# Moving the bounds' matmuls, one evacuation and the norms of a fused attention and feed-forward kernel

## The chip, the cores and the metric

One core of one Trainium2 chip runs the kernel. The metric is the time on the device of one execution in microseconds; lower is better. The engines are TensorE (PE, its weight loads PEld), VectorE (DVE), ScalarE (ACT), GpSimd (POOL) and SyncE (SP), which here issues DMAs.

## The reference

Attention over 4 batches and 8 heads with pooled queries, then a normalised feed-forward with a residual:

```python
# q, k, v: (4, 8, 1152, 64) f32;  w_ch1: (512, 2048);  w_ch2: (2048, 512)
q_pool = q.reshape(B, H, S // 2, 2, D).mean(axis=3)
scores = scale * np.matmul(q_pool, k.transpose(0, 1, 3, 2))
attn = np.exp(scores - np.max(scores, axis=-1, keepdims=True))
attn = attn / (np.sum(attn, axis=-1, keepdims=True) + 1e-09)
x = np.matmul(attn, v)            # then (B, 576, 512)
xn = (x - mu) / np.sqrt(var + 1e-06) * g_ln
out = x + np.maximum(xn @ w_ch1, 0.0) @ w_ch2
```

## The kernel before, in words

**Steps.** Two heads of one batch are a pair `p` (16 pairs, 4 to a batch, `HP` = 4), and a pair has 9 steps of 128 query rows against 1152 keys (`C` = 9), so 144 steps `i`, followed by some 20 that only finish. The order in which each engine gets its instructions is written out by hand in `step(i)`: what it calls first stands first in an engine's queue. `early` and `todo` hold what is to be done at the start or at the end of a given step (`pre`, `at`).

**Attention in a step.** `emit_s(i + 1)` computes the next step's scores into a slot of three PSUM banks (line 380 for 1024 keys, 388 for the last 128; the slots of even and odd steps are banks 0 to 2 and 3 to 5). Keys and queries are split into a high and a low fp16 part, so three products are summed. `emit_max` reduces the row maximum (399), `emit_exp` exponentiates (413). In the first batch (`on_pe`, steps 0 to 35) the probabilities stay fp32: TensorE transposes them (446), ScalarE copies them out (452), TensorE multiplies with the values (470), and the 65-row result is turned back (498, `emit_turn`). From step 36 on the probabilities are split into two fp16 parts: `emit_hi` on ScalarE (427), `emit_lo` on VectorE (436) or, in every third step, on GpSimd (254, 434); one transposing DMA on SP (439) turns them, and four steps later TensorE multiplies them with the split values (482). Such a result lies in the third bank of the next step's slot.

**Evacuation.** `evac_pv` gives two closures: `one` takes the reciprocal of the row sums on VectorE (530, or 532 and 533), `two` scales the 64 columns out of PSUM into the row buffer on ScalarE (537). In the first batch `one` goes to `found`, which is run at the start of the next step right after the maximum, and `two` to `scaled_out`, which is run after that step's exponential. Later both go to `evacs`, which `flush` runs after the scores of the step.

**Banks and evacuations.** Two banks (6 and 7) serve everything else: pieces of keys and queries (`prep_k`, `prep_q`), units of the feed-forward and the norms' transposes. `bank()` takes a free one; if there is none it runs `flush()`, which issues all evacuations that wait.

**Bounds and scales.** Each pair needs a power of two for keys, queries and values. `bound` sums absolute values per partition on ScalarE (190). `scales_reduce` puts two closures into `reds`, one to a step: `one` transposes the accumulators (206), and in the next step's flush VectorE takes the maximum (209) and multiplies it with the identity (210); `two` spreads it over the partitions by a small matmul (215), and in the flush after that `scales` makes the factors (235 to 250). Both matmuls write the third bank of the next step's slot, other columns. From step 36 on `step` issues them right after the next scores and the split, ahead of the product with the values, the pieces and the unit.

**Preparations.** While pair `p - 1` runs, pair `p` is prepared; with `i0` the first step of pair `p - 1`, the loads go out near `i0`, the bounds at `i0` to `i0 + 2`, the reduction at `i0 + 2` or `i0 + 3`, and the pieces from `i0 + 4` on, one a step, in the order of `PREPS` (each is transposed on TensorE, lines 294, 298, 323, 333; then high part on ScalarE, 283 or 308, low part on VectorE, 280 or 303). From pair 6 on the queries of two pairs are prepared together with the even pair, which then has two more pieces. Raw keys and raw values have one buffer each. All loads go through SP's queue, in order.

**Feed-forward.** When a batch's 128-row tile is complete, `evacuated` appends it to `norms`; `norm(i)` takes one a step: mean and variance on VectorE (563, 564), the scaling on GpSimd (569 to 575), and two steps later four transposes on TensorE (581) with evacuations on ScalarE and VectorE (587, 588). Two normalised tiles give `units`, one of which TensorE does in each step (`some_units`): first layer 24 matmuls (618, evacuated at 631 and 632), second layer 8 to 12 matmuls (650, evacuated at 663). What is left when step 143 is done makes the tail.

**Order in a step from 36 on:** maximum, `found`, scores of the next step, `flush`, exponential, high part, low part of the step before, `norm`, one of `reds`, product with the values, piece, unit, `todo`.

## Time and profile before

| | us |
|---|---|
| median of 3 runs (lowest, highest) | 913.89 (908.51, 914.88) |
| the profiled execution | 909.41 |
| its span, first to last instruction | 907.4 |
| mean granted TensorE clock | 0.983 |
| TensorE busy | 826.9 (91%) |
| VectorE busy | 624.7 (69%) |
| ScalarE busy | 569.6 (63%) |
| GpSimd busy | 361.6 (40%) |

The profile is of one execution. Busy time is the share of the span in which the engine ran an instruction; a wait is idle time ahead of an instruction, put down to the semaphore that came last. Steps 0 to 35 run from 16.0 to 203.7 us, 36 to 53 to 303.9, 54 to 142 to 778.2, counted from one maximum to the next; the rest is the last step and the tail.

### The profile page before, as it was taken

The page shows a single profiled execution, that of the slowest core. Times are in us where ns is not written, and L with a number is a line of the kernel's source. Part 1 is how long each engine was busy: PE and PEld are TensorE (multiplying, and loading weights), DVE is VectorE, ACT ScalarE, POOL GpSimd, SP SyncE. Part 2 cuts the span into 40 slices and gives each one's busy share as a digit, 9 for nine tenths or more (in the row PEclk, how much of TensorE's full clock was granted, in tenths as well). Part 3 has the DMA queues.
Part 4 walks back from the last instruction along what each step waited for, and adds up shares of the span by engine and source line. Part 5 has one row for each costly group of instructions (what it writes and reads, how often), then busy time and mean ns, then how long its engine had stood idle before and what let it go on. Part 6 is the DMA issues. An engine that isn't in the chain of part 4 may idle for free.

```text
span 907.4 us, 21663 instructions
## 1 busy us (share of the span) xinstructions
PE 826.9 (91%) x9180; PEld 584.8 (64%) x9180; DVE 624.7 (69%) x1087; ACT 569.6 (63%) x850; POOL 361.6 (40%) x324
## 2 busy tenths in 40 slices
PE   8998897998789988797999999898989999999997
PEld 6787776776546564654666666466657576766764
DVE  3688989797877786576777777877777777641211
ACT  4998696887657756566766667576767766511110
POOL 3020927257859726262633334444624342400000
PEclk9999899899999999898999999999999999999999
DMA  7374425304676877776796969587888876600001
GB/s 191 136 213 127 148 84 163 119 26 94 121 163 129 185 140 143 164 155 136 147 176 114 194 134 186 111 179 132 162 157 147 162 129 131 131 20 12 13 12 24
DMA packets 276017, 115.97 MB, mean 128 GB/s; under 512 B 259280, under 2 KB 259280, under 8 KB 275920
## 3 DMA queue, kind: packets, MB, share of 16 engines
q1 hardware_dynamic: 275568, 113.70, 59.2%
q8 instruction: 72, 1.18, 0.6%
q10 hardware_dynamic: 352, 0.88, 0.4%
q14 instruction: 25, 0.20, 0.1%
HBM read 46.14 MB, written 4.72 MB: 56 GB/s over the span
## 4 chain that ended last, share of the span: by engine, by line
PE 40%; DVE 31%; ACT 16%; DMA 5%; issue 5%; POOL 2%; SPq 0%; ACTq 0%; POOLq 0%; DVEq 0%
PE psum L650 12%; PE psum L618 10%; DVE mx L399 9%; DVE hl L436 6%; ACT pe L413 4%; PE psum L470 4%; PE psum L482 4%; DMA pt<-hl 3%; PE psum L380 3%; DVE ht L632 3%; PE psum L446 2%; DVE stage L111 2%; ACT ht L631 2%; ACT qt L283 2%; DVE dg L210 1%
## 5 line engine op out<-in xcount | busy, mean ns | idle before, releaser
L413 ACT ACTIVATE pe<-psum,nb,sc 128x1152 f32<-128x1152 f32 x144 | 188.9, 1312 | 36.8 <-DVE nb L404 26.1
L399 DVE TENSOR_REDUCE mx<-psum 128x1 f32<-128x1152 f32 x144 | 194.3, 1349 | 25.3 <-PE psum L482 12.9
L650 PE MATMUL psum<-wsl,ht 128*128 128x512 f16 x864 | 197.8, 381 | 1.9 <-DVE xb L663 0.8
L618 PEld LDWEIGHTS <-wsl 128*128 128x128 f16 x1920 | 172.6, 99 | 24.1 <-issue 4.4
L618 PE MATMUL psum<-xn,wsl 128*128 128x256 f16 x1536 | 180.3, 276 | 1.5 <-DVE ht L632 0.8
L650 PEld LDWEIGHTS <-ht 128*128 128x128 f16 x864 | 83.0, 98 | 92.3 <-issue 4.7
L427 ACT ACTIVATE hl<-pe 128x1152 f16<-128x1152 f32 x108 | 125.7, 1163 | 9.8 <-DMA pt<-hl 6.5
L380 PE MATMUL psum<-kt,qt 64*128 64x512 f16 (+1 forms) x960 | 121.8, 380 | 3.2 <-ACT pe L413 2.3
L482 PE MATMUL psum<-vt,pt 128*128 128x65 f16 (+1 forms) x3240 | 118.4, 194 | 0.0
L482 PEld LDWEIGHTS <-pt 128*128 128x128 f16 (+1 forms) x3240 | 110.3, 101 | 2.3 <-issue 0.2
L436 DVE SCALAR_TENSOR_TENSOR hl<-pe,hl 128x1152 f16<-128x1152 f32 x72 | 108.8, 1512 | 3.5 <-ACT hl L427 3.5
L537 ACT ACTIVATE xb<-psum,r 128x64 f32<-128x64 f32 x128 | 39.4, 308 | 113.7 <-DVE r L533 110.3
L254 POOL TENSOR_SCALAR pe<-pe 128x1152 f32<-128x1152 f32 x36 | 42.1, 1169 | 163.0 <-ACT hl L427 151.0
L632 DVE SCALAR_TENSOR_TENSOR ht<-psum,ht 128x512 f16<-128x512 f32 x72 | 49.7, 690 | 75.1 <-ACT ht L631 74.7
L631 ACT ACTIVATE ht<-psum 128x512 f16<-128x512 f32 x72 | 42.8, 594 | 88.9 <-PE psum L618 88.7
L434 POOL TENSOR_TENSOR hl<-pe,hl 128x1152 f16<-128x1152 f32 x36 | 86.4, 2399 | 3.0
L470 PE MATMUL psum<-pt,vt 128*65 128x128 f32 (+1 forms) x720 | 80.5, 269 | 1.4 <-DVE qt L280 1.4
L470 PEld LDWEIGHTS psum<-pt,vt 128*65 128x65 f32 x720 | 74.6, 142 | 1.8 <-DVE qt L280 1.8
L380 PEld LDWEIGHTS <-qt 64*128 64x128 f16 (+1 forms) x960 | 34.3, 96 | 55.7 <-issue 36.2
L388 PEld LDWEIGHTS <-qt 128*128 128x128 f16 (+1 forms) x320 | 17.9, 99 | 72.5 <-issue 72.0
L280 DVE SCALAR_TENSOR_TENSOR qt<-psum,s,qt 128x512 f16<-128x512 f32 (+2 forms) x43 | 28.5, 663 | 42.7 <-ACT qt L283 42.7
L388 PE MATMUL psum<-kt,qt 128*128 128x128 f16 (+1 forms) x320 | 41.4, 226 | 12.1 <-ACT xb L537 10.5
(119 smaller groups left out, 1021.9 us busy)
## 6 DMA issues: line engine op xcount, KB each, us to landing
stage<-in_moe_w_ch_dram SPq DMA_DIRECT2D x32, 512.0 KB, 5.1
kr<-in_k_dram SPq DMA_DIRECT2D x16, 576.0 KB, 4.7
qraw<-in_q_dram SPq DMA_DIRECT2D x31, 288.0 KB, 5.0
vr<-in_v_dram SPq DMA_DIRECT2D x15, 576.0 KB, 4.9
out_dram<-xb SPq DMA_DIRECT2D x32, 128.0 KB, 2.4
pt<-hl SPq DMA_TRANSPOSE x108, 4.6
kr<-in_k_dram SPq DMA_DIRECT2D x16, 64.0 KB, 4.3
vr<-in_v_dram ACTq DMA_DIRECT2D x1, 576.0 KB, 6.8
```

What stands on the lines that cost most here:

```text
L380: nc.tensor.matmul(out=sp[o:o + w, c0:c0 + 512], lhsT=qt[r:r + 64, qa, c:c + w], rhs=kt[r:r + 64, ka, h], start=(a == 0), stop=(a == 2),)
L399: nc.vector.tensor_reduce(mx, st["s"], axis=AX.X, op=ALU.max)
L413: nc.scalar.activation(out=st["pe"], in_=st["s"], func=ACTF.Exp, scale=pair[i // C]["sc"][:, 0:1], bias=st["nb"],)
L427: nc.scalar.activation(out=hl[:, 0], in_=st["pe"], func=ACTF.Copy, scale=2.0 ** 15)
L434: nc.gpsimd.tensor_tensor(hl[:, 1], st["pe"], hl[:, 0], op=ALU.subtract)
L436: nc.vector.scalar_tensor_tensor(hl[:, 1], st["pe"], 2.0 ** 15, hl[:, 0], op0=ALU.mult, op1=ALU.subtract)
L470: nc.tensor.matmul(out=ps[0:65, q0:q0 + w], lhsT=vt[:, h, c], rhs=pt[:, 128 * u + q0:128 * u + q0 + w], start=(u == 0), stop=(u == C - 1),)
L482: nc.tensor.matmul(out=dst[:, 0:n], lhsT=lhsT, rhs=rhs, start=(u == 0 and lhsT is hi and n == 65), stop=(u == C - 1 and lhsT is lo), skip_ ...
L618: nc.tensor.matmul(out=ps[:, o:o + n], lhsT=wsl[:, 8 * w + cc, wa, f * 128:f * 128 + 128], rhs=xn[:, xa * KD + cc, 0:n], start=(m == 0), s ...
L631: lambda: nc.scalar.activation(out=hi, in_=pv, func=ACTF.Relu),
L632: lambda: nc.vector.scalar_tensor_tensor(lo, pv, 0.0, hi, op0=ALU.max, op1=ALU.subtract),
L650: nc.tensor.matmul(out=ps, lhsT=hv[0][:, ha, f, t * 128:t * 128 + 128], rhs=wsl[:, 8 * w + 4 + f // 2, wa, (f % 2) * DM:(f % 2) * DM + DM] ...
```

## The change

- In `all_max`, the product of line 210 is one operation on the PSUM block: maximum of the block's n columns and `mx`, times the identity. As `mx` is the row's maximum the value is the same.
- In the first batch `two` runs on VectorE, and directly behind `one`; `scaled_out` is gone.
- From step 54 on (`JOINT * C`), a bound's matmul is issued behind the feed-forward's unit of its step instead of ahead of the product with the values.
- `norm` leaves a batch's third and fourth tile, and the half tiles, until the sixth step of a pair or later.
- Pair 5 prepares its second key piece last, two steps later than before, and its last two query pieces stay where they were. From pair 6 on, an even pair's last two query pieces come one step later.
- Pair 6's keys are loaded two steps later, its values one, and its key bound is one step later. The other pairs' times stay.

```diff
--- before.py
+++ after.py
@@ -207,7 +207,9 @@
 
             def evac():
                 nc.vector.tensor_reduce(mx[0:n], ps[0:n], axis=AX.X, op=ALU.max)
-                nc.vector.tensor_scalar(dg[0:n, 0:n], ident[0:n, 0:n], mx[0:n], None, op0=ALU.mult)
+                nc.vector.scalar_tensor_tensor(
+                    dg[0:n, 0:n], ps[0:n, 0:n], mx[0:n], ident[0:n, 0:n], op0=ALU.max, op1=ALU.mult
+                )
             return evac
 
         def two():
@@ -339,6 +341,8 @@
     PREPS = ((prep_k, 0), (prep_k, 2), (prep_q, 0), (prep_k, 1), (prep_q, 1), (prep_q, 2))
 
     def preps_of(p):
+        if p == JOINT - 1:
+            return PREPS[:3] + PREPS[4:] + PREPS[3:4]
         if p < JOINT:
             return PREPS
         if p % 2:
@@ -487,7 +491,7 @@
                     )
         return ps
 
-    turned, scaled_out = deque(), deque()
+    turned = deque()
 
     def emit_turn(n, ot, i):
 
@@ -497,8 +501,7 @@
         for h, q0, w in parts:
             nc.tensor.transpose(ps[0:w, 65 * h:65 * h + 65], ot[:, q0:q0 + w], ident[0:65, 0:65])
         one, two = evac_pv(n, ps)
-        found.append(one)
-        scaled_out.extend((two, lambda: evacuated(n)))
+        found.extend((one, two, lambda: evacuated(n)))
 
     pv_slot = [0]
     xb, xh = {}, {}
@@ -534,10 +537,11 @@
 
         def two():
             for u in range(m):
-                nc.scalar.activation(
-                    out=x[:, 64 * u:64 * u + 64], in_=ps[o:o + n, 65 * u:65 * u + 64],
-                    func=ACTF.Copy, scale=r[:, u:u + 1],
-                )
+                src, dst = ps[o:o + n, 65 * u:65 * u + 64], x[:, 64 * u:64 * u + 64]
+                if on_pe(i):
+                    nc.vector.tensor_scalar(dst, src, r[:, u:u + 1], None, op0=ALU.mult)
+                else:
+                    nc.scalar.activation(out=dst, in_=src, func=ACTF.Copy, scale=r[:, u:u + 1])
 
         return one, two
 
@@ -832,10 +836,10 @@
         if old:
             lk = max(i0 - 1, 0)
         else:
-            lk = i0 - 2 if p % 2 or not ahead else i0 - 3
+            lk = i0 - 3 * ahead + p % 2
         at(lk, load, p, "k", nc.sync)
-        at(i0 - ahead, load, p, "v", nc.sync)
-        at(i0 + 1 if old else i0, bound, p, "k")
+        at(i0 if old else i0 + 1 - 2 * ahead, load, p, "v", nc.sync)
+        at(i0 if ahead else i0 + 1, bound, p, "k")
         if p == 1:
             upper = (64, 64)
             pre(0, behind_scales)
@@ -864,8 +868,8 @@
         for n in range(2):
             at(i0 + 5 + (2 * n if late else n), take_v, p, n)
         for n, (fn, u) in enumerate(preps_of(p)):
-            if p == JOINT - 1 and n > 3:
-                n -= 1
+            if u > 2:
+                n += 1
             pre(i0 + 4 + n + late, lambda fn=fn, p=p, u=u: preps.append((fn, p, u)))
 
     for m in range(32):
@@ -917,7 +921,10 @@
 
         if not norms or norms[0][1] % 2 == 0 and norms[0][0] != "h" and not room["xn"]:
             return
-        b, t = norms.popleft()
+        b, t = norms[0]
+        if i < NSTEP and (b == "h" or t > 1) and i % C < 5:
+            return
+        norms.popleft()
         st = {}
         if b == "h":
             x = xh[t][:, 0]
@@ -1012,8 +1019,6 @@
             a_piece(i)
             a_prep()
             emit_exp(i)
-        while scaled_out:
-            scaled_out.popleft()()
         if i + 1 < NSTEP:
             emit_s(i + 1)
             pv_slot[0] = i + 1
@@ -1042,7 +1047,7 @@
             emit_t(i)
             if reds:
                 found.append(reds.popleft()())
-        elif reds:
+        elif reds and i < JOINT * C:
             evacs.append(reds.popleft()())
         while turned:
             n, ot = turned.popleft()
@@ -1053,6 +1058,8 @@
             for _ in range(max(len(preps), 1)):
                 a_prep()
             some_units(i)
+            if reds and i >= JOINT * C:
+                evacs.append(reds.popleft()())
         for fn, a in todo.pop(i, ()):
             fn(*a)
```

## Rows read from the trace of the kernel before

**Rows 1.** Busy time by stretch: us; PE, PEld, DVE, ACT, POOL; clock; DMA share; GB/s.
```profile
16.00:203.70 187.70, 168.28 (x1666) 140.53 (x1664) 155.38 (x253) 156.67 (x290) 68.23 (x58) 0.96 0.41 129
203.70:303.90 100.20, 86.95 (x993) 58.80 (x992) 76.71 (x130) 67.30 (x93) 78.60 (x60) 0.98 0.65 131
303.90:778.20 474.30, 434.82 (x5314) 288.94 (x5313) 351.00 (x623) 320.60 (x425) 200.42 (x179) 0.99 0.79 152
```
**Rows 2.** Groups by line, 16 to 203.7, TensorE: busy, mean ns | idle before, releasers.
```profile
L388 PE MATMUL psum<-kt,qt 128*128 128x128 f16 (+1 forms) x80 | 10.4, 226 | 11.0 <-ACT xb L537 9.4 <-ACT xh L537 1.5
```
**Rows 3.** Timeline, 77 to 80: start, us, engine, line, operation [idle before, releaser].
```profile
77.77 1.31 ACT L413 ACTIVATE pe<-psum,nb,sc 128x1152 f32<-128x1152 f32 x1
...
78.98 0.30 ACT L537 ACTIVATE xb<-psum,r 128x64 f32<-128x64 f32 x1
...
79.33 0.27 PE L388 MATMUL psum<-kt,qt 128*128 128x128 f16 x2 [0.91 <-ACT xb L537]
```
**Rows 4.** Groups by line and shape, whole span.
```profile
L537 ACT ACTIVATE xb<-psum,r 128x64 f32<-128x64 f32 x128 | 39.4, 308 | 113.7 <-DVE r L533 110.3 <-PE psum L618 1.9 <-DVE r L530 1.2
...
L303 DVE SCALAR_TENSOR_TENSOR kt<-psum,s,kt 64x256 f16<-64x256 f32 x16 | 7.9, 491 | 9.7 <-ACT kt L308 9.5
```
**Rows 5.** Line 210 alone: ns shortest/median/longest, first and last start, forms.
```profile
L210 DVE TENSOR_SCALAR dg<-ident,mx x20: 201/217/2385, 11.0 to 713.5; 3x3 f32<-3x3 f32 x13, 1x1 f32<-1x1 f32 x4, 2x2 f32<-2x2 f32 x3
```
**Rows 6.** TensorE's waits, 303.9 to 778.2: us in total, times, longest.
```profile
PE psum L215 <- DVE dg L210: 10.8, 6, 2.6
PE psum L298 <- DVE kt L280: 5.6, 5, 1.3
PE psum L206 <- ACT kt L190: 5.1, 3, 3.9
```
**Rows 7.** Groups by line and shape, 303.9 to 778.2, TensorE.
```profile
L581 PE MATMUL psum<-ident,xs 128*128 128x128 f32 x36 | 5.6, 279 | 8.6 <-DVE qt L280 3.6 <-DVE xb L663 2.7 <-DVE kt L280 2.3
```
**Rows 8.** Timeline, 468 to 476, steps 83 and 84.
```profile
468.74 2.78 PE L618 MATMUL psum<-xn,wsl 128*128 128x256 f16 x24
...
469.53 1.35 DVE L399 TENSOR_REDUCE mx<-psum 128x1 f32<-128x1152 f32 x1
...
471.35 2.38 DVE L210 TENSOR_SCALAR dg<-ident,mx 3x3 f32<-3x3 f32 x1
471.36 2.36 POOL L434 TENSOR_TENSOR hl<-pe,hl 128x1152 f16<-128x1152 f32 x1
...
473.79 0.38 PE L215 MATMUL psum<-dg,ones 3*128 3x3 f32 x2 [1.27 <-DVE dg L210]
...
475.59 1.35 DVE L399 TENSOR_REDUCE mx<-psum 128x1 f32<-128x1152 f32 x1
```
**Rows 9.** Timeline, 212 to 213.2, step 37 to 38.
```profile
212.39 0.28 PE L388 MATMUL psum<-kt,qt 128*128 128x128 f16 x2
...
212.60 0.38 PE L215 MATMUL psum<-dg,ones 1*128 1x1 f32 x2
...
213.02 1.36 DVE L399 TENSOR_REDUCE mx<-psum 128x1 f32<-128x1152 f32 x1 [0.87 <-PE psum L215]
```
**Rows 10.** Timeline, 481 to 486, step 86.
```profile
481.89 1.34 DVE L399 TENSOR_REDUCE mx<-psum 128x1 f32<-128x1152 f32 x1
...
485.64 0.44 PE L298 MATMUL psum<-ident,kr 128*128 128x128 f32 x2 [1.26 <-DVE kt L280]
```
**Rows 11.** Timeline, 252 to 254, TensorE, step 43.
```profile
252.58 0.90 PE L323 MATMUL psum<-ident,qraw 64*128 64x64 f32 x6 [4.18 <-DVE kt L280]
```
**Rows 12.** Timeline, 266 to 270, SP's queue.
```profile
268.11 0.57 SPq L127 DMA_DIRECT2D vr<-in_v_dram  x1
```
**Rows 13.** Timeline, 261 to 276, ScalarE.
```profile
273.70 1.15 ACT L190 ACTIVATE kt<-vr 128x1152 f16<-128x1152 f32 x1
```
**Rows 14.** Busy time of two short stretches; columns as in rows 1.
```profile
95.98:104.21 8.23, 5.83 (x53) 4.90 (x51) 8.16 (x7) 4.56 (x10) 7.92 (x6) 1.00 0.75 251
424.00:431.00 7.00, 7.00 (x58) 5.10 (x57) 2.88 (x10) 3.68 (x6) 2.90 (x2) 0.57 0.58 110
```

## The prediction

> **What bounds the kernel now.** I read the stretches first, then TensorE's waits in each, then single steps in order of time. The stretches [rows 1] show TensorE busy for 168.3 of 187.7 us while the first batch is attended, 87.0 of 100.2 in the change-over and 434.8 of 474.3 in the long middle, where a feed-forward unit goes into each step. VectorE has 351 of 474 us in the middle, so TensorE sets the time, and its idle time (19.4, 13.2 and 39.5 us) is what an edit can win. An edit that relieves another engine wins nothing unless TensorE waited for it.
>
> Whom TensorE waits for: in the first batch, 11.0 us at line 388, for ScalarE's scaled copy of an output [rows 2]. In the middle, 10.8 us ahead of the bounds' second matmul (line 215) for the small product of line 210, 5.1 us ahead of their transposition (206) for the bound's accumulator and 5.6 us ahead of the short key piece (298) [rows 6]; and 8.6 us ahead of the norms' transposes (581) for a free bank [rows 7].
>
> The sum is made against the profiled execution (909.41 us, span 907.4). The median of the runs, 913.89, is 0.5% above that; I take the sum off the median.
>
> **Part 1, the first batch's evacuation on VectorE.** 40 copies (36 steps, 4 of them with two) leave ScalarE at 0.31 us each [rows 4] and go onto VectorE right behind the reciprocal. Price there: an operation from PSUM over 256 columns takes 0.49 us [rows 4], the smallest ones 0.20 [rows 5]; 64 columns lie nearer the lower row, so 0.25 us, 10 us in all. What the wait is worth: at 77.77 ScalarE starts the exponential, at 78.98 the copy, and only then does the last piece of the scores (line 388) run, at 79.33 [rows 3]. Without the copy behind the exponential that piece runs 0.91 us earlier, but the next thing in TensorE's queue, the transposes of the probabilities, still needs the exponential, which ends at 79.08. So a wait of 0.9 gives back 0.25 to 0.6, not 0.9. At 0.9 or so a wait, the 11.0 us are some twelve; at 0.45 each, -5.5 us. Where VectorE is full the added 0.25 us is on the path: in one such step it has 8.16 of 8.23 us [rows 14], and about seven steps look like it, +1.5. Sum -4; ends -11 (every wait gone) and +10 (all 40 copies on the path).
>
> **Part 2, the bounds.** Two edits: the 3x3 product reads PSUM, and from step 54 on a bound's matmuls stand behind the feed-forward's unit. The product is 0.2 us at best and 2.39 at worst [rows 5]; at 471.35 it starts with GpSimd's subtraction and ends with it, after 2.38 us, and TensorE stands until 473.79 [rows 8]. The new form has no row. Its ends are 0.2 (the unhindered product) and 2.4 (hindered as now); I take 0.25, the end it is nearer to, as one of its two operands now comes from PSUM, where GpSimd's subtraction has nothing. The Trainium skill, "SBUF — State Buffer", section "Who interferes with whom", says which operations meet: GpSimd and VectorE share one pair of SBUF ports, which a VectorE operation takes in a two-port mode or with two SBUF tensors. By it the price is the low end, and no run here shows that.
>
> With both edits the 10.8 and 5.1 us go, nine pairs with two places each. What is late next is the row maximum of the next step. At 212.39 the scores' last matmul starts and runs to 212.67, the bound's matmul in the same bank runs from 212.60 to 212.98, and the maximum starts at 213.02, named as waiting for line 215, though it reads other columns [rows 9]. So the maximum waits for whatever TensorE writes into that bank ahead of it in the program. Behind the unit that is one unit later: 24 matmuls, 2.8 us, and 0.4 for the bound's own [rows 8]. Queued behind the maximum on VectorE are the reciprocals, the unit's low half and the key pieces' low halves, which free TensorE's two banks.
>
> One pair worked out (steps 83 to 86). Before: maxima at 469.53, 475.59 [rows 8] and 481.89, and the short key piece gets its bank at 485.64 [rows 10]. After: the unit from 468.74 ends at about 471.3, so the maximum starts at 471.6 instead of 469.53; the next bound's matmul no longer waits, the next unit ends near 476.2, and the maximum starts at 476.5 instead of 475.59. The step behind is shorter on VectorE by some 0.9 us (the scales come last, and meet less of GpSimd), so the third maximum comes at 481.5 to 482.3 and the key piece again at about 485.6. TensorE's 1.3 us at line 215 turn up at line 298: net 0. By the same steps, pairs with a longer wait at 215, or one at 206 too (8, 9, 12, 14), gain 2.7, 1.5, 1.3 and 2.8. In odd pairs (7, 11, 13, 15; 9 has no unit in that step) the change also moves the even pair's last two query pieces one step on, so that the last one wants its bank in the step whose maximum is now held; I get 1.9 us of new wait and 2 us lost a pair, +8. Sum of part 2: about 0; ends -15.9 and +20 (rivals A and B).
>
> **Part 3, norms away from prepared keys.** Their work stays: 36 transposes in the middle. What goes is the collision of three users of two banks: of the 8.6 us [rows 7], the 2.7 behind line 663 and nearly half of the 3.6, where a norm's second tile met the third query piece, and most of the 2.3, where the later tiles met key pieces; together -6. The stalls of the first batch end (with the bound's wait) stand right ahead of a stretch whose granted clock is 0.57 on the mean, 424 to 431 [rows 14], so most of it at 1.2 GHz instead of 2.4; if they go, another -1. Against it, the half tiles' norm now meets a key and a query piece, +1. No unit should be missing for it: a batch's first half gives 16 units (9 in the first batch), and the late half comes 2 to 3 steps later. Sum -6; ends -10.5 and 0.
>
> **Part 4, pair 5's and 6's preparations.** A stall of 4.18 us, where two pieces and a norm met [rows 11], mostly goes: -3.4. For that, pair 5's second key piece moves two steps on, and as raw keys have one buffer, pair 6's keys are loaded two steps later and its values one. These loads stand on SP behind the transposing DMA of the step before, which waits for GpSimd's subtraction; before, the values' load was issued at 268.11 [rows 12] and their bound ran at 273.70 without a wait [rows 13]. Now the keys' load takes that place and their bound follows one step behind, so ScalarE stands up to 4 us ahead of an exponential, and TensorE behind it for a part: +2.4. Sum -1; ends -4 and +4.
>
> **Sum.** -4 + 0 - 6 - 1 = -11, so 913.9 - 11 = 903 us.
>
> **Rivals.**
> A, the bounds' waits go and nothing takes their place: VectorE has a quarter of the middle free [rows 1], so it may make up a held maximum before its banks are wanted. Then part 2 is -15, the total -26: 888. Against it: line 298 already waits 5.6 us for VectorE, two steps behind the bounds.
> B, slower: the held maximum decides. 18 times it starts behind a unit; if VectorE makes up nothing, each pair's key piece comes 2.2 us later than now, nine pairs +20, total +9: 923. It decides once the hold (up to 3.2 us, twice a pair) is more than VectorE's free time between the bounds and the key piece, some 2 us. For it: rows 9 and the odd pairs; against: the pair worked out, where it just breaks even. The Trainium skill, "PSUM — Partial Sum Buffer", section "PSUM bank collisions raise a hardware error", has any two engines kept apart by bank, not by address. Rows 9 agree, and by that rule the edit cannot escape the hold, which is B's 923 if no slack takes it up.
> C, the saved time is waited away elsewhere: the DMA engines' share is 0.79 in the middle [rows 1], and a step that comes earlier finds its transposed probabilities or a load late. Most of parts 1, 3 and 4 goes back: -3, 911.
>
> **How the numbers follow.** Forecast 0.50 (own range 896 to 909), A 0.20, C 0.15, B 0.15. A measurement of this kernel tells about 1%, 9 us, from no change: two thirds of the forecast's share and all of A are faster by more, 0.53; the rest of the forecast and C are within, 0.32; B is slower, 0.15. The range 887 to 918 holds A and C and leaves out most of B.
>
> **What would show it.** Right: line 388 no longer waits in the first batch, and the transposes of the probabilities wait a little more; line 210 near 0.25 us; no wait ahead of 215 and 206 in the middle; the maximum named as waiting for 215 or 206, up to 3 us, some ten times or more; more than 5.6 us ahead of 298 and new wait ahead of 333; under 4 ahead of 581; ScalarE standing near pair 6's bounds. Wrong: line 298 unchanged with 215's wait gone (A), VectorE full all through the first batch (part 1 a loss), or more units left for the tail (part 3).

## The result, and the profile after

The changed kernel takes 921.84 us (median of 7 runs, 919.68 to 922.55) against 912.70 for the kernel before beside it (7 runs, 908.10 to 916.35): a ratio of 1.0104, interval 1.0074 to 1.0133. It is about 1% slower; forecast was 903, 1% faster, with a range up to 918. So the forecast missed in sign and range. The time that came is near the one given for rival B, 923, but it is made up of other terms; that it fits is luck, as the last part of the account below shows.

In the changed kernel the lines ahead of 200 keep their numbers, 206 to 210 too, then 215 is 217, 298 is 300, 380 is 384, 388 is 392, 399 is 403, 413 is 417, 446 is 450, 537 is 542 on VectorE and 544 on ScalarE, 581 is 585, 618 is 622, 632 is 636. In kernels with the new product and without the edit of pairs 5 and 6, lines behind 210 stand 2 further down than before (399 is 401, 413 is 415, 482 is 484, 581 is 583, 618 is 620, 632 is 634).

The stretches after, cut at the same steps as [rows 1] (columns as there):

```profile
18.00:205.10 187.10, 169.08 (x1667) 138.85 (x1666) 164.43 (x288) 149.03 (x254) 65.89 (x57) 0.98 0.42 129
205.10:306.70 101.60, 87.70 (x994) 59.78 (x992) 74.06 (x135) 66.99 (x89) 77.33 (x59) 0.97 0.67 130
306.70:791.40 484.70, 435.26 (x5314) 288.61 (x5313) 339.91 (x623) 320.39 (x425) 207.61 (x179) 0.99 0.78 148
```

The first batch is 0.6 us shorter, the change-over 1.4 longer, the middle 10.4 longer. In the middle TensorE is busy as long as before (435.3 against 434.8 us): what grew is its idle time, from 39.5 to 49.4 us. So the loss is waiting, and the middle is the place to look. A stretch of one profile is one execution, though: the run only_evac below, whose program in the middle is that of the kernel before, took 468.8 us there instead of 474.3. A difference of 5 us between two profiles of the middle shows nothing by itself; the times decide.

TensorE's waits in the middle, changed kernel (line waited at, whom for: us in total, times, longest):

```profile
PE psum L296 <- DVE qt L282: 7.6, 5, 1.5
PE psum L300 <- DVE kt L282: 7.6, 8, 1.2
PE psum L384 <- ACT pe L417: 7.6, 9, 1.6
PE psum L622 <- DVE ht L636: 4.7, 9, 1.4
PE psum L335 <- DVE qt L282: 4.6, 3, 1.9
...
PE psum L585 <- DVE qt L282: 2.1, 2, 1.9
...
PE psum L585 <- DVE kt L282: 1.2, 1, 1.2
```

Everything that the prediction wanted to go has gone: no wait of the 10.8 and 5.1 us of [rows 6] is left (line 217 waits 1.2 us, once, for another engine), and the norms' transposes wait 3.3 us where they waited 8.6 [rows 7]. In their place stand VectorE's evacuations (lines 282 and 636), and the exponential (417). VectorE itself was not busier: it was made to wait. Its group for the row maximum in the middle, changed kernel (busy, mean ns of one, idle time ahead and what ended it):

```profile
L403 DVE TENSOR_REDUCE mx<-psum 128x1 f32<-128x1152 f32 x89 | 120.2, 1350 | 45.6 <-PE psum L217 23.9 <-PE psum L206 9.0 <-PE psum L486 6.6
```

32.9 us of wait for the bounds' two matmuls, nine times for 217 and five for 206, where the kernel before has less than 0.1 in its middle: that is the held maximum of [rows 9], in every pair. One pair in order of time shows how it is handed on (changed kernel, steps 83 to 85, start and us):

```profile
469.61 1.35 DVE L440 SCALAR_TENSOR_TENSOR hl<-pe,hl 128x1152 f16<-128x1152 f32 x1
...
470.45 2.78 PE L622 MATMUL psum<-xn,wsl 128*128 128x256 f16 x24
...
473.07 0.27 PE L206 MATMUL psum<-ident,acc 128*3 128x128 f32 x1
...
473.38 1.36 DVE L403 TENSOR_REDUCE mx<-psum 128x1 f32<-128x1152 f32 x1 [2.42 <-PE psum L206]
...
475.40 0.31 ACT L544 ACTIVATE xb<-psum,r 128x64 f32<-128x64 f32 x1 [3.35 <-DVE r L536]
475.62 0.59 ACT L635 ACTIVATE ht<-psum 128x512 f16<-128x512 f32 x1
476.24 0.69 DVE L636 SCALAR_TENSOR_TENSOR ht<-psum,ht 128x512 f16<-128x512 f32 x1 [0.93 <-ACT ht L635]
476.85 0.27 DVE L209 TENSOR_REDUCE mx<-psum 3x1 f32<-3x128 f32 x1
477.15 0.21 DVE L210 SCALAR_TENSOR_TENSOR dg<-psum,mx,ident 3x3 f32<-3x3 f32 x1
477.39 1.31 ACT L417 ACTIVATE pe<-psum,nb,sc 128x1152 f32<-128x1152 f32 x1 [1.19 <-DVE dg L210]
...
478.24 1.36 DVE L403 TENSOR_REDUCE mx<-psum 128x1 f32<-128x1152 f32 x1 [0.88 <-PE psum L217]
...
478.76 0.61 PE L384 MATMUL psum<-kt,qt 64*128 64x512 f16 x4 [0.56 <-ACT pe L417]
```

VectorE is done with the split at 470.96 and stands for 2.42 us, though the scores that it is to reduce ended at 469.79: it waits for the unit (470.45 to 473.23) and the bound's matmul behind it. All that is queued behind it on VectorE comes later by that: the reciprocal, for which ScalarE's copy (line 544) waits 3.35 us; behind that copy the two halves of the unit (635 and 636, at 476.24); and then the bound's maximum and product. The exponential (417) starts at 477.39, behind line 210, though its own maximum ended at 474.74, and TensorE waits 0.56 us for it at 478.76. The 3x3 product (line 210) is 0.21 us, where it was 2.39 in [rows 5].

So the hold has a second half, on ScalarE: the exponential reads the bank that VectorE reads the bound from. ScalarE's waits in the middle, changed kernel:

```profile
ACT pe L417 <- DVE dg L210: 15.3, 9, 3.6
...
ACT pe L417 <- DVE red L237: 9.8, 9, 2.9
```

That is 25.1 us, twice in each of the nine pairs. No kernel here that has the matmuls ahead of the product with the values shows such a wait, and every one that has them behind the unit in that bank does. In only_behind_unit, where line 210 does not read PSUM, the exponential waits for line 209 instead (12.1 us, nine times), the last reading of that bank. Moving the matmul also moved these readings, since evacuations run in the order in which they were put up: now they come behind the unit's low half. The prediction priced the held maximum and not the held exponential.

### The profile page after: what moved, and what is told of

The parts are those of the page before. It is cut to its first block, busy times and chain, and to the rows that moved or that the text cites. A ratio compares the mean times of both kernels' runs of the same rounds, so it can differ in the third digit from the quotient of the medians.

```text
span 920.6 us, 21644 instructions
## 1 busy us (share of the span) xinstructions
PE 830.5 (90%) x9180; PEld 584.7 (64%) x9180; DVE 620.0 (67%) x1127; ACT 561.6 (61%) x810; POOL 366.2 (40%) x324
## 3 DMA queue, kind: packets, MB, share of 16 engines
HBM read 46.14 MB, written 4.72 MB: 55 GB/s over the span
## 4 chain that ended last, share of the span: by engine, by line
PE 45%; DVE 30%; ACT 12%; POOL 5%; issue 5%; DMA 2%; SPq 1%; ACTq 0%; POOLq 0%; DVEq 0%
PE psum L622 14%; PE psum L654 13%; DVE mx L403 9%; DVE hl L440 4%; PE psum L486 4%; PE psum L384 4%; ACT pe L417 3%; PE psum L474 3%; DVE stage L111 3%; PE psum L450 2%; DVE ht L636 2%; DVE wsl L111 2%; POOL hl L438 2%; DVE qt L282 2%; DVE kt L282 2%
## 5 line engine op out<-in xcount | busy, mean ns | idle before, releaser
L636 DVE SCALAR_TENSOR_TENSOR ht<-psum,ht 128x512 f16<-128x512 f32 x72 | 49.6, 689 | 78.2 <-ACT ht L635 78.0
L544 ACT ACTIVATE xb<-psum,r 128x64 f32<-128x64 f32 x96 | 29.7, 309 | 106.5 <-DVE r L536 104.1
L450 PE MATMUL psum<-ident,pe 128*128 128x128 f32 x324 | 43.7, 281 | 10.4 <-ACT pe L417 10.4
```

The source lines that it names most:

```text
L636: lambda: nc.vector.scalar_tensor_tensor(lo, pv, 0.0, hi, op0=ALU.max, op1=ALU.subtract),
```

## The experiments

Five edits make the change. Here they are called: the product (line 210 from PSUM), behind the unit (place of the bounds' matmuls), the copies (first batch's evacuation), the norms (kept off early steps; the query pieces' shift is told apart), and pairs 5 and 6. Ratios are to the kernel before on the same chip, with a 95% interval.

### Which of the five turns the sum

```diff
 undo_behind_unit, on the changed kernel (only_behind_unit is its reverse, on the kernel before)
-        elif reds and i < JOINT * C:
+        elif reds:
             evacs.append(reds.popleft()())
...
             some_units(i)
-            if reds and i >= JOINT * C:
-                evacs.append(reds.popleft()())
 ahead_of_unit, on the changed kernel
+            if reds and i >= JOINT * C:
+                evacs.append(reds.popleft()())
             some_units(i)
-            if reds and i >= JOINT * C:
-                evacs.append(reds.popleft()())
 only_product, on the kernel before
-                nc.vector.tensor_scalar(dg[0:n, 0:n], ident[0:n, 0:n], mx[0:n], None, op0=ALU.mult)
+                nc.vector.scalar_tensor_tensor(
+                    dg[0:n, 0:n], ps[0:n, 0:n], mx[0:n], ident[0:n, 0:n], op0=ALU.max, op1=ALU.mult
+                )
```

> The changed kernel with one edit undone: from step 54 on a bound's matmul stands again ahead of the product with the values. The 3x3 product stays in its new form. Theory 1 (the bound's matmul behind the unit holds the next row maximum, since it writes the maximum's bank, and that is the whole loss of the middle): 905 to 912 us, 10 to 16 below the changed kernel, idle time ahead of the maxima back near 25 us, steps 54 to 142 at 468 to 474 us. Theory 2 (the moved query pieces and norms cost it): within 4 us of the changed kernel, 918 to 922, the middle still above 480. Theory 3 (VectorE's added copies and pair 6's late loads, ahead of the middle, cost it): the same as theory 2, with steps 0 to 53 as in the changed kernel.

> The changed kernel, but from step 54 on a bound's matmul stands between the pieces and the feed-forward's unit: behind the product with the values, ahead of the unit. Theory 1 (a held maximum costs by the work that stands ahead of the bound's matmul): the hold shrinks by a unit's 2.8 us, so 902 to 910 us, as fast as with the matmuls ahead of the product or 1 to 4 us better, since the 3x3 product has more time to be done. Rival (any place behind the product with the values holds the maximum long enough to cost, because the product itself stands ahead of it): 914 to 919. Theory 2 (moved pieces and norms): 918 to 922.

> The kernel before with one edit: from step 54 on a bound's matmul stands behind the feed-forward's unit. The 3x3 product stays as before. Theory 1: the loss of the middle shows without any of the other edits: 920 to 928 us against 913, steps 54 to 142 near 484. Theory 2 (moved pieces and norms, alone or together with the hold): 910 to 915, the middle at 471 to 476.

> The kernel before with one edit: the 3x3 product reads the PSUM block. Line 210 goes to 0.21 us everywhere. Prediction's working of part 2: the wait ahead of the bounds' second matmul is 10.8 us in the middle and has this product behind it, so 4 to 8 us less, 905 to 909. Rival (VectorE's wait behind GpSimd only moves to the next operation, or the small product was late for another reason): 912 to 914, the wait ahead of line 215 still above 6 us.

| | us, median | ratio | middle, us |
|---|---|---|---|
| undo_behind_unit | 900.79 | 0.9884 (0.9821 to 0.9947) | 462.0 |
| ahead_of_unit | 898.56 | 0.9853 (0.9788 to 0.9918) | 461.7 |
| only_behind_unit | 916.13 | 1.0036 (1.0003 to 1.0068) | 476.9 |
| only_product | 899.55 | 0.9875 (0.9818 to 0.9931) | 462.2 |

The middle is counted from step 54's maximum to step 143's; it was 474.3 us before and 484.7 in the changed kernel. Undoing one edit takes 21 us off the changed kernel and makes it faster than the kernel before; this and ahead_of_unit came out below the times that theory 1 expected (905 and 902 at the least). Theories 2 and 3 fall: the moved pieces, norms, copies and loads are all still in, and the middle is 462.0. The rival of ahead_of_unit falls too: what makes the hold too long is the unit, not the product with the values. only_behind_unit fits no theory as it stands: 916.1 is below theory 1's range and just above theory 2's. Beside the old product the place costs only 0.36%, as it also ends most of the wait ahead of line 215, 10.8 us before and 2.3 in this kernel.

The second finding was not looked for: one 3x3 product, by itself, is worth 11.5 us, 1.25%, more than the expected 4 to 8. TensorE's waits in the middle with the product alone:

```profile
PE psum L206 <- ACT kt L190: 5.5, 2, 5.1
...
PE psum L217 <- DVE dg L210: 3.0, 3, 2.2
```

10.8 us are 3.0, and the small product no longer takes VectorE 12.0 us (nine of 1.33 us) but 1.9. The 11.5 us are the difference of the medians; the row of waits accounts for 7.8 of them. The maxima of that kernel stand as little as before, 17.7 us:

```profile
L401 DVE TENSOR_REDUCE mx<-psum 128x1 f32<-128x1152 f32 x90 | 121.4, 1349 | 17.7 <-PE psum L484 11.2 <-ACT xb L539 5.6 <-ACT xh L539 0.6
```

### The pair of edits, the query pieces, the bank, and the copies

```diff
 product_and_behind: the kernel before with the product and behind the unit, as above
 no_query_shift, on the changed kernel
-            if u > 2:
-                n += 1
 other_bank, on the changed kernel
-            u = this[0] if on_pe(this[0]) else pv_slot[0]
+            u = this[0] if on_pe(this[0]) or this[0] >= JOINT * C else pv_slot[0]
 only_evac, on the kernel before (and two goes to found, behind one)
-                nc.scalar.activation(
-                    out=x[:, 64 * u:64 * u + 64], in_=ps[o:o + n, 65 * u:65 * u + 64],
-                    func=ACTF.Copy, scale=r[:, u:u + 1],
-                )
+                src, dst = ps[o:o + n, 65 * u:65 * u + 64], x[:, 64 * u:64 * u + 64]
+                if on_pe(i):
+                    nc.vector.tensor_scalar(dst, src, r[:, u:u + 1], None, op0=ALU.mult)
+                else:
+                    nc.scalar.activation(out=dst, in_=src, func=ACTF.Copy, scale=r[:, u:u + 1])
```

> The kernel before with both edits of part 2 and nothing else: the 3x3 product reads PSUM, and from step 54 on a bound's matmul stands behind the unit. So far: the product alone 899.6, behind the unit alone 916.1, both in the changed kernel 921.8. Theory 1 in its plain form (the hold alone makes the loss; both edits remove the same wait ahead of line 215, so the gain of the product is had once): 914 to 917, steps 54 to 142 at 474 to 477 us. Theory 1 with the query pieces (the hold costs some 13 us, and the query pieces moved into the held steps another 8): the same here, and the rest of the loss in the run without the query shift. Rival (the two edits add up: -11.5 and +5): 904 to 906.

> The changed kernel, but an even pair's last two query pieces stay in their steps of before; the norms wait as changed. Prediction's working of the odd pairs: the moved pieces cost 8 us in all, as the last one wants its bank where the maximum is held: 913 to 916, idle time ahead of the query pieces (lines 296 and 335) down from 12 to under 5 us. Rival (the pieces only show the hold, and it turns up elsewhere without them; or the norms that now share their steps with the pieces collide): 919 to 923.

> The changed kernel, with the bounds' matmuls still behind the unit but from step 54 on written into the third bank of the running step's slot, whose maximum and exponential are done, and not of the next step's. What reads them on VectorE follows at the same place as before. Theory 1 (the maximum is held because it reads a bank that TensorE still has to write): the wait of the maxima for line 217 goes, 900 to 908 us, steps 54 to 142 at 462 to 470. Rival (the late product and its readers on VectorE cost the time, not the held maximum): 917 to 922, and the waits ahead of the pieces stay.

> The kernel before with one edit: the first batch's scaled copies on VectorE, behind the reciprocal. Prediction: 4 us less, ends -11 and +10. By the profile of the changed kernel, where steps 0 to 35 took 187.1 us against 187.7: 910 to 912, within 1 us of before, the 11 us of wait at line 388 replaced by some 10 us ahead of the transposes of the probabilities (line 446). Rival (VectorE is full in the last steps of the batch, and the added copies are on the path there): 914 to 918.

product_and_behind: 913.53 us, ratio 1.0002 (0.9974 to 1.0029), middle 476.9. The plain form of theory 1 holds, with the middle in its range and the time 0.5 us under it: the hold gives back the whole gain of the product, 1.0002 / 0.9875 or 1.3%. Its own maxima and waits in the middle:

```profile
L401 DVE TENSOR_REDUCE mx<-psum 128x1 f32<-128x1152 f32 x89 | 120.2, 1351 | 39.0 <-PE psum L217 17.4 <-PE psum L206 8.9 <-PE psum L484 6.8
```

```profile
PE psum L620 <- DVE ht L634: 7.9, 9, 1.4
...
PE psum L382 <- ACT pe L415: 5.0, 6, 1.4
PE psum L583 <- DVE kt L282: 4.1, 2, 2.1
```

21.3 us more of held maximum than with the product alone (39.0 against 17.7); the middle is 14.7 us longer. The exponentials wait 23.7 us for the bound's readings, and not at all with the product alone. Of TensorE's new waits the plainest is at line 620, nine times: in six of the nine pairs, up to 1.4 us each, the unit of the step behind the second hold finds its bank taken, since VectorE does the last unit's low half (634) late; the other three are 0.2 us a step later. The prediction looked for it one step later, at the key piece.

no_query_shift: 920.65, ratio 1.0091 (1.0061 to 1.0121): 1.2 us less than the changed kernel, not 6 to 9. The rival holds. The query pieces' waits go down as expected (line 335 waits 2.8 us in all, where it had 4.6 for line 282 alone), but the unit's line 622 then waits 9.5 us for line 636, where it had 4.7: the stall is the hold's and falls on what comes next.

other_bank: 908.56, ratio 0.9939 (0.9915 to 0.9963), 13 us less than the changed kernel with the matmuls still behind the unit. The maxima no longer wait for 217 or 206, nor the exponentials for the bound's readings:

```profile
L403 DVE TENSOR_REDUCE mx<-psum 128x1 f32<-128x1152 f32 x90 | 121.4, 1349 | 22.3 <-PE psum L486 15.5 <-ACT xb L544 6.0 <-ACT xh L544 0.7
```

```profile
PE psum L486 <- DVE dg L210: 15.8, 9, 3.4
...
PE psum L486 <- DVE red L237: 2.4, 9, 0.3
```

It does not reach 900 because the next product with the values writes that bank and now waits 15.8 us, nine times, for VectorE's reading of the bound. The middle is 468.6, within what theory 1 expected, and the total just over its upper end. That the shared bank makes most of the loss is shown by this run. How the loss divides between the held maximum and the held exponential is not, since the edit takes both away. In both banks that were tried somebody waits for the bound.

only_evac: 913.00, ratio 0.9985 (0.9953 to 1.0016), first batch 187.9 against 187.7 us: no gain that can be told from none. The time lies between the two expectations. The waits are as expected: 2.3 us at line 388 and 11.3 at line 446.

### The other three edits without the hold, and the place once more

```diff
 product_norms, on only_product
-        b, t = norms.popleft()
+        b, t = norms[0]
+        if i < NSTEP and (b == "h" or t > 1) and i % C < 5:
+            return
+        norms.popleft()
 product_pairs56, on only_product
+        if p == JOINT - 1:
+            return PREPS[:3] + PREPS[4:] + PREPS[3:4]
...
-            lk = i0 - 2 if p % 2 or not ahead else i0 - 3
+            lk = i0 - 3 * ahead + p % 2
...
-        at(i0 - ahead, load, p, "v", nc.sync)
-        at(i0 + 1 if old else i0, bound, p, "k")
+        at(i0 if old else i0 + 1 - 2 * ahead, load, p, "v", nc.sync)
+        at(i0 if ahead else i0 + 1, bound, p, "k")
 product_evac: only_product with only_evac's edit
 product_ahead: only_product with ahead_of_unit's place
```

> The kernel before with the 3x3 product from PSUM (899.6 us alone) and the norms kept off a pair's first five steps; the query pieces stay in their steps of before. Prediction's part 3: 6 us less from the norms' transposes, whose wait ahead of line 583 was 9.2 us with the product alone: 893 to 896. Rival (the waits ahead of the transposes go, but work that was done earlier now comes later and is waited for elsewhere, as at line 382 for the exponential): 898 to 902.

> The kernel before with the 3x3 product from PSUM and pair 5's and 6's changed preparations. Prediction's part 4: 1 us less (3.4 won at the stall of line 325, 2.4 lost behind the later loads), ends -4 and +4: 897 to 900. Rival (the later loads cost ScalarE's stand in full): 901 to 904. Steps 36 to 53 tell it in the trace: 99 to 100 against 103.5 us with the product alone, or 104 to 107.

> The kernel before with the 3x3 product from PSUM and the first batch's copies on VectorE. Prediction's part 1: 4 us less, 895 to 896. By the run of the copies alone (913.0 against 914.5) and its trace, where the wait of line 388 came back at line 446: 898 to 900, steps 0 to 35 at 187 to 188 us. Rival (a full VectorE): 902 or more.

> The kernel before with the 3x3 product from PSUM, and from step 54 on a bound's matmul between the pieces and the unit. In the changed kernel this place gave 898.6 against 900.8 with the matmul ahead of the product with the values. Theory 1 (a hold that is short enough is taken up by VectorE's slack, and the product with the values no longer waits behind a bound's matmul for line 210 and line 190): 895 to 898. Rival (it is no better than ahead of the product): 899 to 901.

| on top of the product | us, median | ratio |
|---|---|---|
| product_norms | 901.91 | 0.9892 (0.9859 to 0.9925) |
| product_pairs56 | 904.68 | 0.9912 (0.9879 to 0.9945) |
| product_evac | 902.22 | 0.9892 (0.9849 to 0.9935) |
| product_ahead | 898.48 | 0.9854 (0.9817 to 0.9892) |

None of the three gains anything that can be told over the product's 0.9875. The norms' run falls to the rival; pairs 5 and 6 come out 0.7 us above theirs, and in neither range in the stretch named: steps 36 to 53 take 103.1 us against 103.5 with the product alone. The copies' time is in the rival's range, their steps 0 to 35 (187.8 us) in the other; the run says only that there is no gain. The stall of [rows 11] is gone, and five steps later stand these two (product_pairs56, TensorE):

```profile
273.10 0.84 PE L384 MATMUL psum<-kt,qt 64*64 64x512 f16 x12 [1.62 <-ACT pe L417]
...
276.80 0.37 PE L206 MATMUL psum<-ident,acc 128*3 128x128 f32 x1 [2.62 <-ACT kt L190]
```

1.62 and 2.62 us, together 4.2, for ScalarE, which waited for the later keys (line 190 started at 270.39 after 4.04 us of standing) and had three bounds to do in this step. What was won is paid back.

product_ahead and ahead_of_unit are the fastest of all that ran, 898.5 us, faster than both kernels. They can't be told from the product alone (0.9875, interval 0.9818 to 0.9931), so most of their gain is the product's; product_ahead's time lies between its two expectations. ahead_of_unit has all the other edits and product_ahead none, and they stand at 0.9853 and 0.9854: without the hold the copies, the norms and the preparations together are worth nothing that can be told.

### Why the hold costs more in the changed kernel

```diff
 behind_norms, behind_pairs56, behind_evac: product_and_behind with one of the three edits above
 ahead_of_pieces, on only_product
-        elif reds:
+        elif reds and i < JOINT * C:
             evacs.append(reds.popleft()())
...
+            if reds and i >= JOINT * C:
+                evacs.append(reds.popleft()())
             for _ in range(max(len(preps), 1)):
                 a_prep()
             some_units(i)
```

> The kernel before with the 3x3 product from PSUM, the bounds' matmuls behind the unit (both: 913.5 us), and the norms kept off a pair's first five steps. Theory 1a (the waiting norms use up what slack VectorE has behind the held maximum, and make the rest of the loss): 917 to 922. Theory 1b (the rest comes from another edit): 912 to 915.

> The kernel before with the 3x3 product from PSUM, the bounds' matmuls behind the unit, and pair 5's and 6's changed preparations. They lie in steps 36 to 57 and touch one pair: 912 to 916. Rival (the later loads of pair 6 shift what follows): 917 to 922, and the loss stands in pairs 4 to 6.

> The kernel before with the 3x3 product from PSUM, the bounds' matmuls behind the unit, and the first batch's copies on VectorE. Nothing of the copies is left after step 36: 913 to 915. Rival (what the first batch leaves undone is done later beside the hold): 917 or more.

> The kernel before with the 3x3 product from PSUM, and from step 54 on a bound's matmul behind the product with the values and ahead of the pieces. Places so far, beside the new product: ahead of the product with the values 899.6, behind the pieces 898.5, behind the unit 913.5. If the cost grows with the work ahead of the matmul only once it is more than the slack: 897 to 900. Rival (a wait for line 210 or 190 at this place stands ahead of pieces and unit as it did ahead of the product): 899 to 902.

| | us, median | ratio |
|---|---|---|
| behind_norms | 916.63 | 1.0055 (1.0030 to 1.0080) |
| behind_pairs56 | 913.91 | 1.0018 (0.9990 to 1.0045) |
| behind_evac | 913.45 | 1.0020 (0.9994 to 1.0046) |
| ahead_of_pieces | 900.24 | 0.9866 (0.9828 to 0.9904) |

Over product_and_behind (1.0002) the norms add 0.53%, pairs 5 and 6 0.16%, the copies 0.18%, the query shift 0.13% (changed kernel against no_query_shift). The sum is 1.0%, and the changed kernel stands at 1.04%. Only the norms' part is larger than its uncertainty (some 0.37%, from the two intervals), and the norms' time is just under what theory 1a expected. The middles agree: the four kernels with the matmuls behind the unit in the shared bank and without the norms' edit take 476.0 to 477.2 us there, the three with it (behind_norms, no_query_shift, the changed kernel) 480.8 to 484.7. How the rest of the 1.0% divides is open. In the middle of behind_norms the waits of key pieces ahead of the transposes do go:

```profile
PE psum L620 <- DVE ht L634: 9.9, 13, 1.4
PE psum L300 <- DVE kt L282: 7.3, 8, 0.9
PE psum L382 <- ACT pe L415: 7.1, 9, 1.6
...
PE psum L652 <- DVE xb L665: 2.1, 3, 1.1
...
PE psum L583 <- DVE kt L282: 1.2, 1, 1.2
```

Line 583's wait for key pieces is 1.2 us where product_and_behind has 4.1; but 620 goes from 7.9 to 9.9, 382 from 5.0 to 7.1, 300 from 5.6 to 7.3 and 652 from 1.0 to 2.1. One place of it (behind_norms, steps 115 and 116):

```profile
648.54 3.53 POOL L436 TENSOR_TENSOR hl<-pe,hl 128x1152 f16<-128x1152 f32 x1
...
652.11 1.31 ACT L415 ACTIVATE pe<-psum,nb,sc 128x1152 f32<-128x1152 f32 x1 [6.48 <-POOL hl L436]
...
653.47 0.82 PE L382 MATMUL psum<-kt,qt 64*128 64x512 f16 x6 [1.62 <-ACT pe L415]
```

GpSimd's split takes 3.53 us, the exponential waits for it and TensorE for the exponential. That step is 9.35 us long here and 4.72 in product_and_behind, which had its long step earlier (8.81 us in step 112, now 5.34). GpSimd gets to the split late: from 639.96 on it works without a pause, through a norm's scaling and a pair's values and queries, and in product_and_behind it had done the norm and the values by 639.8 and stood before the queries. Over the middle the exponential's waits for the split are these in behind_norms and then in product_and_behind:

```profile
ACT pe L415 <- POOL hl L436: 19.4, 5, 6.5
```

```profile
ACT pe L415 <- POOL hl L436: 8.1, 2, 4.4
```

So these rows point to GpSimd, and not to the slack on VectorE of which theory 1a speaks. Without the hold the same waits grow as well (9.0 us with the product alone, 20.1 in product_norms) and the time doesn't by any amount that can be told. Why they cost time only beside the hold stays open; no run takes it apart.

The place, beside the new product: ahead of the product with the values 0.9875, behind it and ahead of the pieces 0.9866, behind the pieces 0.9854, behind the unit 1.0002. Of the four places three cost nothing that can be told, the fourth 1.3%, some 12 us. The 900.2 us ahead of the pieces decide nothing between the two expectations, which meet there.

### What makes the product fast

```diff
 product_two_sbuf, on the kernel before
-                nc.vector.tensor_scalar(dg[0:n, 0:n], ident[0:n, 0:n], mx[0:n], None, op0=ALU.mult)
+                nc.vector.scalar_tensor_tensor(
+                    dg[0:n, 0:n], ident[0:n, 0:n], mx[0:n], ident[0:n, 0:n], op0=ALU.mult, op1=ALU.mult
+                )
```

> The kernel before with the 3x3 product as one operation of the new kind (two tensors and a scalar), but both tensors are the identity in SBUF: identity times maximum times identity, the same value. If it is the operand in PSUM that keeps the product clear of GpSimd: line 210 again up to 2.4 us in some of its 20 runs, the wait ahead of line 215 near 10 us, 911 to 915. If it is the kind of instruction (the old one, a tensor and a scalar, has another way of reading): 0.2 us in all 20, 898 to 902.

912.80 us, ratio 0.9998 (0.9967 to 1.0028): nothing is won, and the wait ahead of the bounds' second matmul is back at 9.8 us in the middle. Line 210 in only_product, then in this kernel (ns min/median/max, first and last start in us):

```profile
L210 DVE SCALAR_TENSOR_TENSOR dg<-psum,mx,ident x20: 204/207/208, 10.8 to 704.4; 3x3 f32<-3x3 f32 x13, 1x1 f32<-1x1 f32 x4, 2x2 f32<-2x2 f32 x3
```

```profile
L210 DVE SCALAR_TENSOR_TENSOR dg<-ident,mx x20: 206/208/2377, 12.1 to 719.6; 3x3 f32<-3x3 f32 x13, 1x1 f32<-1x1 f32 x4, 2x2 f32<-2x2 f32 x3
```

```profile
327.00 2.37 POOL L436 TENSOR_TENSOR hl<-pe,hl 128x1152 f16<-128x1152 f32 x1
...
327.64 1.73 DVE L210 SCALAR_TENSOR_TENSOR dg<-ident,mx 3x3 f32<-3x3 f32 x1
```

The same instruction with one tensor in PSUM takes 0.204 to 0.208 us in all 20 places; with both in SBUF it ends with GpSimd's subtraction at 329.37, as the old one did in [rows 8]. So it is the operand in PSUM that makes the new product fast, and not the kind of instruction. The Trainium skill, "SBUF — State Buffer", section "Who interferes with whom", says that a VectorE instruction with two SBUF inputs contends with a GpSimd one that reads SBUF, and one with a single SBUF input, outside the two-port modes, does not. The runs agree, with 2.377 against 0.208 us. The old product had only one tensor in SBUF and a scalar, and was held too (2.385 us, [rows 5]); what holds that form no run here takes apart.

## Why the prediction was wrong, point by point

What failed is the step from a wait to a gain. Parts 1, 3 and 4 forecast -11 us for waits that end; most of those waits did end, and others came in their place. Nearly all signs that were named for being right came: no wait ahead of 215 and 206 for the bound, more than 5.6 us ahead of 298 (7.6), new wait ahead of 333, under 4 ahead of 581 (3.3), ScalarE standing at pair 6's keys (5.3 us). They told where the waits would go and not what they cost.

**Part 2, the bounds (forecast 0, ends -15.9 and +20).** The price of the product, 0.25 us, was right (0.21). The hold was foreseen, and its size (2.42 us in the pair shown, up to 3.2 forecast). The pair worked out was right as well: from the maximum of step 83 to that of 87 the kernel before takes 23.4 us and product_and_behind 23.2, "net 0". Taken over all nine pairs the two edits alone come to 1.0002, so "about 0" stands for them, by luck in part: the working left out the held exponential, and it put too much on the moved query pieces. What the working had wrong is where the parts lie. By the starts of the maxima, in steps 54 to 134, product_and_behind against before, by the pair prepared:

| pair prepared | forecast | measured |
|---|---|---|
| 8, 9, 12, 14 | -8.3 | -4.6 |
| 7, 11, 13, 15 | +8 (with the query pieces moved) | +8.1 (without) |
| 10 | 0 | -0.8 |

The odd pairs lose by the hold itself, and the moved pieces cost 1.2 us in all, not 8. The gain of the first group is not shown: only_evac, with nothing changed in these steps, has -6.1 there; in the odd pairs it has +0.3. The step that missed the point of the whole change is that the two edits were priced as one: the sum hides -1.25% for the product and +1.27% for the place, some 12 us each. Nothing in the working asked what the product would be worth with the matmuls left where they were, though it took away up to 2.2 us a time, 10.1 us of VectorE's time and 7.8 of TensorE's waits in the middle.

**Part 3, the norms (forecast -6; measured +5 beside the hold, and about +2 without it, which is within the uncertainty).** This is the step that failed by most. The waits at line 581 that were to go did go, 5.3 of 8.6 us in the changed kernel. But "together -6" took the end of a wait for a gain. The same transposes, GpSimd's scaling and the evacuations come later beside other work, the exponential waits for GpSimd's split 19.4 us instead of 8.1, and TensorE's idle time in the middle rose by 6.9 us when the norms alone were moved beside the hold (42.7 to 49.6).

**Part 1, the copies (forecast -4, measured -1.4 alone, interval -4.3 to +1.5).** The swap at the wait was foreseen: line 392 waits 2.4 us for VectorE where 388 waited 11.0, and the transposes of the probabilities wait 10.4 where they waited 2.7. The first batch, changed kernel, then before:

```profile
PE psum L450 <- ACT pe L417: 10.4, 16, 1.0
...
PE psum L392 <- DVE xb L542: 1.7, 4, 0.4
```

```profile
PE psum L446 <- ACT pe L413: 2.7, 4, 0.9
```

The term that failed is what the swap gives back: 8.6 us went at the one line and 7.7 came at the other, so 0.9 us and not 5.5. The copy on VectorE takes 0.28 us, near the 0.25. The cost on VectorE was charged to steps with a full VectorE only. In a step with room on VectorE (changed kernel, step 8):

```profile
55.96 2.69 POOL L171 TENSOR_TENSOR qraw<-qraw 64x1152 f32<-64x1152 f32 x1 [29.14 <-ACT pe L417]
...
56.17 3.02 DVE L111 SCALAR_TENSOR_TENSOR wsl<-stage 128x512 int32<-128x512 int32 x1
```

Two copies came ahead of the weights' split (line 111), and GpSimd's operation came 0.6 us earlier in the step, so that the split now starts 0.2 us after it instead of ahead of it and takes 3.02 us instead of 0.69; the step is 6.87 us long where it was 4.95, and that is half of the expected gain. The interval of the copies alone still reaches the -4.

**Part 4, pairs 5 and 6 (forecast -1).** The stall went (forecast -3.4); TensorE's standing behind the later loads was 4.2 us and not 2.4. The time over the product alone, +0.4%, is within the uncertainty.

**Sum and rivals.** -4 + 0 - 6 - 1 became, in the kernel's own setting, about +2, +1, +5 and +1. Only the norms' +5 is clear of the noise by itself. Rival B's time came by other terms than its own, so by luck: it put part 2 at +20 and left the other parts at -11, while part 2 came to about +1 and the others to about +8. The hold is there and costs 1.3%, but it only takes back the product's gain. The rest is what rival C says, that saved time is waited away elsewhere, applied to parts 1, 3 and 4; C's own reason, late DMAs, is not what the waits name. Rival A fell: VectorE's free quarter did not take up all of the hold. Its 888 was out of reach even without the hold: the best place gave 898.5.

## What to carry to other kernels

Where two edits remove the same wait, price each alone before pricing the pair: here the small one (an operand from PSUM) had all the gain, and the large one (a new place) gave it back. Where a matmul shares a PSUM bank with a result that other engines want, ask of each of them what it waits for, the matmul and its readers: here VectorE's maximum waited for the matmul and ScalarE's exponential for its readers. In this kernel three places ahead of the unit cost nothing, and the one behind its 2.8 us cost 1.3%. A wait that ends is worth only what the chain behind it gives: three edits removed named waits of 4 to 9 us each, and nothing of it reached the total.

## What the runs showed that was not expected

A VectorE instruction of nine elements took up to 2.39 us beside GpSimd and cost this kernel 1.25%, and its busy time did not tell that it was blocked. The trace shows it as work.

The start of step 0 is not the same in all profiled executions, though the kernels issue the same work ahead of it: 15.8 to 16.7 us in twelve of the nineteen, 17.3 to 18.8 in seven, the changed kernel among them (18.0). Six of the seven have the bounds' matmuls behind the unit, as eight of the nineteen do, though that edit acts only from step 54 on. Windows 12 to 16 us of only_product and product_two_sbuf (columns as in [rows 1]):

```profile
12.00:16.00 4.00, 3.24 (x41) 2.11 (x40) 2.49 (x9) 1.52 (x3) 3.34 (x4) 1.00 0.25 92
```

```profile
12.00:16.00 4.00, 3.63 (x22) 3.17 (x23) 2.22 (x10) 1.63 (x3) 1.92 (x3) 0.50 0.40 118
```

In the second TensorE was granted 0.50, the lower level of 1.2 GHz, and did 22 matmuls where the first did 41. In this window all seven late profiles have a grant of 0.50 to 0.70; the changed kernel has 0.50, the kernel before 1.00. The later start is 2 of the 13.2 us by which the spans of before and after differ (907.4 and 920.6), and none of the middle. What decides it in an execution was not tried.
